# Attention between the products of an MLP: stages emitted job by job, and by pairs of jobs with shared PSUM banks

## The chip, the cores and the metric

The kernel runs on one core of a Trainium2 chip. The metric is the device time of one execution in microseconds, the median of three runs. TensorE (PE) multiplies matrices into PSUM banks, VectorE (DVE) and ScalarE (ACT) read them, GpSimd (POOL) works on SBUF alone, and SyncE (SP) issues most loads and stores.

## The reference

Three parts, one after the other. q, k and v are (4, 8, 576, 64), that is 4 batches of 8 heads; the token matrix has 2304 rows of 512.

```python
# attention: a coarse one on means of 4 positions, plus a local one in a band
out_d = sm_attn(q_d, k_d, v_d)              # q_d, k_d, v_d: mean over 4 positions, 144 of them
out_up = np.repeat(out_d, 4, axis=2)
mask = np.abs(pos[:, None] - pos[None, :]) < 4
scores = np.where(mask, scale * q @ k.T, -1e9)
x = out_up + softmax(scores) @ v
# MLP: 512 -> 2048 -> 512
h = x @ w_in
g = np.maximum(h, 0.0) + np.log1p(np.exp(-np.abs(h)))
x = g @ w_out
# mixture of 8 experts: each token goes to the one with the highest logit
out[mask] = gate_w * (np.maximum(x[mask] @ w1[e], 0.0) @ w2[e])
```

## The kernel before

**Tiling.** The MLP goes over six blocks `n` of 384 tokens, each with 16 chunks `c` of 128 hidden columns. `mlp_H(n, c)` makes the hidden chunk in one PSUM bank `ph` (12 products of 128x128 by 128x384, since both operands are split into a high and a low part; block 0 uses four float32 products). ScalarE takes Abs, Exp and Ln of it, `mlp_g` makes `g` on VectorE and splits it, and `mlp_Y` adds 12 products into the four banks `py`, three iterations later (`step_Y(3)`). `split_wi` and `split_wo` split the weights for the next iteration on ScalarE and GpSimd. Behind block 5 follow the experts, which the change doesn't touch.

**Attention** is cut into 64 jobs, 16 for each batch: four times a `Down` job (the coarse attention of two heads) and a `Local` job (192 positions of the band, two heads), then eight `Local` jobs. Each job has six stages: `st_T` (transposes of q and k, on VectorE from batch 1 on; also issues loads for later jobs), `st_S` (scores into a bank `pS`, L204 to L216 and L303 to L320; VectorE masks and takes the maximum), `st_E` (exponentials on ScalarE), `st_N` (normalising, VectorE and GpSimd), `st_Ta` (transposes into a bank `pA`, VectorE copies it out) and `st_PV` (values into a bank `pO`, L245 to L253 and L341 to L369; the result is copied to `od` by ScalarE for a Down job, and added to `od` by VectorE for a Local job, which writes the MLP's input `xT`).

**Shapes on TensorE.** Local scores are twelve recorded products of 64 rows by 64 columns, Local values twelve of 70 by 64, Down values eight of 72 by 64, Down scores six of 128 by 96. Transposes are of 128 by 70 or 96 by 72. The MLP's are of 128 by 128.

**Order.** A list `pieces` (L393 to L404) holds every stage of every job by steps: at step s the job s starts, job s-2 makes its scores, s-3 its exponentials, s-4 is normalised, s-6 transposed, and s-7 makes its values. Nineteen steps are emitted before the MLP starts. Then `attn_to` emits up to a position in this list twice in each iteration, once behind `mlp_H` and once behind `mlp_Y`; `targets` (L841) says which job's values end in which block. Each block needs the `xT` of its tokens from jobs emitted before.

The order of emission is a priority. A planner with a model of the engines' times sets each engine's instructions in order when the program is built, and may draw one that it thinks ready ahead of one that it thinks not. On the chip every engine keeps that order.

**Banks.** Once the MLP runs, `pa` gives every stage its own bank of the pool `psa` (four banks), which also holds `ph`.

Of the kernel before, what the change touches and what calls it, by code (L numbers as in the profile page):

```python
# [9 lines left out]
F32 = mybir.dt.float32  # L10
# [12 lines left out]
SD = S // FACTOR  # L23
# [9 lines left out]
QD = SD // 3  # L33
# [15 lines left out]
C0 = 3  # L49
CR = 1  # L50
# [5 lines left out]
def band_attention__softplus_mlp__top1_moe(  # L56
# [64 lines left out]
    class Down:  # L121
# [83 lines left out]
        def st_S(self):  # L205
            mx = apool.tile([2 * QD, 3], F32, tag="dmx", name="dmx", bufs=3)
            self.den = apool.tile([2 * QD, 3, 1], F32, tag="dsm", name="dsm", bufs=3)
            ps = pa("pS")
            for i in range(3):
                T.matmul(ps[:2 * QD, i * SD:(i + 1) * SD], self.qbd[:, i, :], self.kT, start=True, stop=True)  # L210
            p3 = ps[:2 * QD, :3 * SD].rearrange("p (i s) -> p i s", i=3)
            V.tensor_reduce(out=mx, in_=p3, axis=AX.X, op=ALU.max, negate=True)
            self.mx, self.p3 = mx, p3
            self.late = not started[0]
            if not self.late:
                self.exps()  # L216
# [28 lines left out]
        def st_PV(self):  # L245
            ps = pa("pO")
            for h, c in pairs(2):
                T.matmul(ps[h * D:(h + 1) * D, :SD], self.vs[:, c, h, :], self.aT[c][:, :, h, :],  # L248
                         start=(c == 0), stop=(c == 1))
            warm(ps)  # L250
            if self.b not in od:
                od[self.b] = apool.tile([128, NPAIR, SD], F32, tag="od", name="od", bufs=1)
            (A.copy if nloc[0] < 99 else V.tensor_copy)(od[self.b][:, self.hp, :], ps[:, :SD])  # L253
# [12 lines left out]
    def pa(name):  # L266

        if not started[0]:
            nps[0] += 1
            if nps[0] % 2:  # L270
                return psy.tile([128, 512], F32, tag="py", name=name)
        return psa.tile([128, 512], F32, tag="pa", name=name)
# [9 lines left out]
    class Local:  # L282
# [20 lines left out]
        def st_S(self):  # L303
            ps = pa("pS")
# [9 lines left out]
            p3 = ps[:, :3 * KW].rearrange("p (i s) -> p i s", i=3)  # L314
# [26 lines left out]
        def st_PV(self):  # L341
            ps = pa("pO")
# [3 lines left out]
            warm(ps)  # L346
            t0 = self.b * S + self.j * TH
# [52 lines left out]
    step_end = {}  # L400
    for s in range(NJ + LAG):
        step_end[s] = sum(1 for x in pieces if x[0] <= s or x[1] < 0)
    pieces.sort(key=lambda x: x[1] >= 0)
    pre_end = [sum(1 for x in pieces if x[0] <= s and (x[1] < 0 or not 0)) for s in range(NJ + LAG)]  # L404
    pos = [0]

    def attn_to(p):
        while pos[0] < min(p, len(pieces)):
            s, n, st = pieces[pos[0]]
            pos[0] += 1  # L410
            with ahead([0, 0, 0, 0, 0, 0][st]):
                (jobs[n].st_T, jobs[n].st_S, jobs[n].st_E, jobs[n].st_N, jobs[n].st_Ta, jobs[n].st_PV)[st]()
            if st == 0:
                if n + 2 < NJ:
                    with ahead(-50):
                        jobs[n + 2].pre()
                with ahead(0):
                    load_after(n)
# [414 lines left out]
    for st in range(12 + LAG):  # L833
        attn_to(pre_end[st])
        if st >= C0 - 5 + LAG:
            conv_to((st - C0 + 5 - LAG) * CR // 4 + 1)
        if st == 9 + LAG:
            split_wi(0, 0)
    started[0] = True
    CB = cpos[0]  # L840
    targets = [23, 32, 44, 56, 63, 63]  # L841
# [13 lines left out]
    for i, (n, c) in enumerate(seq[:NMLP]):  # L855
        if c == 0:
            p0, p1 = pos[0], step_end[targets[n] + LAG]
# [19 lines left out]
        attn_to(p0 + (p1 - p0) * (2 * c + 1) // (28 if n == 0 else 32))  # L877
# [24 lines left out]
        attn_to(p0 + (p1 - p0) * (2 * c + 2) // (28 if n == 0 else 32))  # L902
# [152 lines left out]
```

## Time and profile before

| | |
|---|---|
| median of 3 runs | 796.02 us (795.82 to 797.77) |
| profiled execution | 799.56 us, of it span 797.8 us |
| TensorE busy | 762.2 us (96%), 4917 products |
| VectorE, ScalarE, GpSimd busy | 553.5, 450.8, 469.3 us |
| mean granted clock of TensorE | 0.962 |

The stages can be read from the starts of the products' lines: attention alone to 74.5 us, block 0 of the MLP to 183.6, then blocks 1 to 5 to 262.9, 355.1, 446.1, 520.3 and 586.6, and the experts to the end. Times in a trace count from the start of the span. A group in the view in order of time is a run of instructions of one line; its duration goes to the end of its last instruction, and the next group starts earlier, as products are pipelined. So a group's cost is read from its start to the next group's start.

### The profile page before, as it was taken

Reading aid. Unit: us, or ns where it says so; the run is one execution under the profiler, and the core shown is the slowest. Engines: PE = TensorE matmul, PEld = TensorE weight load, DVE = VectorE, ACT = ScalarE, POOL = GpSimd, SP = SyncE. Lnnn points to the kernel's source line nnn. Section 1 sums busy time; section 2 is a strip of 40 time slices with the busy share of each in tenths; the row PEclk is TensorE's granted clock in tenths of the full one; section 3 lists DMA queues with packets and bytes.
Section 4 is the critical chain, followed back from the end, with each engine's and each line's share of the span. In section 5 each row is a group of like instructions: output and inputs, shape, how many; then the busy total and the mean of one; then the engine's idle time right before and its main releaser. Section 6 shows DMA issues by size and latency. Waiting matters only on the chain.

```text
span 797.8 us, 13867 instructions
## 1 busy us (share of the span) xinstructions
PE 762.2 (96%) x4917; PEld 666.7 (84%) x4918; DVE 553.5 (69%) x1107; ACT 450.8 (57%) x1164; POOL 469.3 (59%) x447
## 2 busy tenths in 40 slices
PE   5997999899999999999999999999999999999995
PEld 5864655578899989899899999999988889889884
DVE  6778999967987587998665665656998285264322
ACT  5734665666476565657565666555665365355332
POOL 3254713656866566876576657666669555555632
PEclk9665999999999999999999999999999999999998
DMA  8757766503300061301000100071012022001002
GB/s 188 153 112 215 231 196 189 119 13 91 62 12 16 24 124 31 72 12 62 2 12 12 52 2 1 1 288 43 1 39 80 21 60 80 0 1 67 14 0 83
DMA packets 111447, 55.46 MB, mean 70 GB/s; under 512 B 89593, under 2 KB 102411, under 8 KB 111371
## 3 DMA queue, kind: packets, MB, share of 16 engines
q1 hardware_dynamic: 111083, 53.98, 25.4%
q8 instruction: 41, 0.67, 0.4%
q10 hardware_dynamic: 288, 0.52, 0.2%
q14 instruction: 35, 0.29, 0.1%
HBM read 45.05 MB, written 9.44 MB: 68 GB/s over the span
## 4 chain that ended last, share of the span: by engine, by line
PE 70%; DVE 16%; issue 4%; DMA 3%; POOL 3%; ACT 2%; SPq 1%; DVEq 0%; ACTq 0%
PE py L622 18%; PE ph L582 17%; PE py L939 11%; PE ph L783 9%; PE pO L344 3%; PE ph L579 3%; PE pS L311 2%; PE pA L336 2%; DVE cva L442 2%; PE pS L210 1%; DVE g L604 1%; DVE xs L764 1%; PE pO L248 1%; DMA vr<-in_v_dram 1%; DVE cva L440 1%
## 5 line engine op out<-in xcount | busy, mean ns | idle before, releaser
L622 PE MATMUL py<-g,wos 128*128 128x384 f32 x1056 | 211.7, 343 | 5.9 <-POOL g L605 2.4
L622 PEld LDWEIGHTS py<-g,wos 128*128 128x128 f32 x1056 | 183.0, 189 | 13.2 <-issue 4.0
L582 PE MATMUL ph<-xT,wis 128*128 128x384 f32 x960 | 183.9, 338 | 0.0
L582 PEld LDWEIGHTS ph<-xT,wis 128*128 128x128 f32 x960 | 166.3, 188 | 2.0 <-issue 0.4
L479 POOL TENSOR_TENSOR wos<-wo,wos 128x512 fp32r<-128x512 f32 x88 | 124.4, 1413 | 42.6 <-ACT wos L478 42.4
L479 POOL TENSOR_TENSOR wis<-wi,wis 128x512 fp32r<-128x512 f32 x80 | 107.3, 1341 | 51.8 <-ACT wis L478 47.5
L588 ACT ACTIVATE ga<-ph 128x384 f32<-128x384 f32 x96 | 46.7, 487 | 77.2 <-PE ph L582 65.2
L603 DVE SCALAR_TENSOR_TENSOR ga<-ph,ga 128x384 f32<-128x384 f32 x88 | 48.3, 549 | 44.8 <-ACT ga L590 44.5
L783 PE MATMUL ph<-xs,ws 128*128 128x384 f32 x378 | 74.3, 337 | 0.9 <-DVE u L788 0.9
L325 ACT ACTIVATE ls<-ls,lst 128x70 f32<-128x70 f32 x144 | 49.3, 344 | 45.4 <-DVE lst L319 33.4
L788 DVE TENSOR_TENSOR u<-ph,u 128x384 f32<-128x384 f32 x60 | 33.2, 555 | 59.1 <-PE ph L783 58.6
L478 ACT CAST wos<-wo 128x512 fp32r<-128x512 f32 x88 | 54.1, 616 | 33.6 <-PE py L622 32.0
L783 PEld LDWEIGHTS ph<-xs,ws 128*128 128x128 f32 x378 | 67.4, 188 | 4.7 <-DVE u L788 1.6
L939 PE MATMUL py<-wos,gs 128*128 128x512 f32 x270 | 68.9, 393 | 0.4 <-POOL gs L794 0.4
L605 DVE TENSOR_TENSOR g<-ga,g 128x384 fp32r<-128x384 f32 x80 | 65.7, 821 | 1.5
L331 POOL TENSOR_TENSOR ls<-ls,lst 128x210 f32<-128x210 f32 x48 | 31.5, 657 | 56.3 <-DVE lst L330 31.2
L604 DVE CAST g<-ga 128x384 fp32r<-128x384 f32 x80 | 57.8, 722 | 4.3 <-PE py L622 0.9
L939 PEld LDWEIGHTS py<-wos,gs 128*128 128x128 f32 x270 | 50.1, 188 | 9.2 <-POOL gs L794 0.8
L479 POOL TENSOR_TENSOR wos<-w2s,wos 128x512 fp32r<-128x512 f32 x24 | 32.7, 1364 | 35.4 <-ACT wos L478 35.4
L590 ACT ACTIVATE ga<-ga 128x384 f32<-128x384 f32 x96 | 50.3, 524 | 2.1
L589 ACT ACTIVATE ga<-ga 128x384 f32<-128x384 f32 x96 | 50.4, 525 | 0.4
L478 ACT CAST wis<-wi 128x512 fp32r<-128x512 f32 x80 | 48.9, 611 | 0.4 <-PE ph L582 0.4
(165 smaller groups left out, 1311.7 us busy)
## 6 DMA issues: line engine op xcount, KB each, us to landing
raw<-in_moe_w_in_dram SPq DMA_DIRECT2D x16, 512.0 KB
raw<-in_moe_w_out_dram SPq DMA_DIRECT2D x16, 512.0 KB
lv<-in_v_dram SPq DMA_DIRECT2D x72, 70.0 KB
vr<-in_v_dram SPq DMA_DIRECT2D x16, 288.0 KB
ydram<-y SPq DMA_DIRECT2D x12, 384.0 KB
yb<-ydram SPq DMA_DIRECT2D x12, 384.0 KB
out_dram<-ob SPq DMA_DIRECT2D x16, 256.0 KB
qr<-in_q_dram SPq DMA_DIRECT2D x48, 72.0 KB
```

The costliest lines, as they stand in the source:

```text
L325: A.activation(s[:, i, :], s[:, i, :], AF.Exp, bias=st[:, 0, i], accum_out=st[:, 1, i])
L478: A.copy(w[:, 0], src)
L479: G.tensor_tensor(out=w[:, 1], in0=src, in1=w[:, 0].bitcast(F32), op=ALU.subtract)
L582: T.matmul(ps[:, :TB], wt[:, w, cc, :], xT[n][:, x, cc, :], start=(i == 0), stop=(i == 3 * CC - 1))
L589: A.activation(a, a, AF.Exp, scale=-1.0)
L590: A.activation(a, a, AF.Ln, bias=1.0)
L603: V.scalar_tensor_tensor(a, ps[:, :TB], 0.0, a, ALU.max, ALU.add)
L604: (A.copy if n < 1 else V.tensor_copy)(g[:, 0, :], a)
L605: (G if n < 1 else V).tensor_tensor(out=g[:, 1, :], in0=a, in1=g[:, 0, :].bitcast(F32), op=ALU.subtract)
L622: T.matmul(yps[n][dc][:, :TB], w[:, a, dsl], g[:, b, :], start=(c == 0 and i == 0), stop=(c == NC1 - 1 and i == 2))
L783: T.matmul(ps[:, :TB], ops[:, w, a, cc, :], xop[p, x][:, l, cc, :], start=i == 0, stop=i == 5)
L939: T.matmul(yps[n][t], g[:, a, t * 128:(t + 1) * 128], w[:, b, :], start=first and c == q and i == 0, stop=last and c == q + NQ and i == 2)
```

## The change

`st_S` and `st_PV` are cut in two: the products stay, and what reads them goes into `st_S2` and `st_PV2`. Up to step 19 the order is the same, with the second halves directly behind the first. From there on a stage's place is given by its pair of jobs (`n // 2`) and a slot: start 0.4, scores 1.0, normalising 1.4, transposing 1.7, values 2.0. At a whole number t come the values of both jobs of pair t-2, the scores of both jobs of pair t-1, then the readers of the values, the readers of the scores and the exponentials. `pa2` gives both jobs of a pair one bank, columns from 0 and from 256: for values always, for scores where both jobs are Local. `ends` replaces `targets`, as slot times at which the blocks begin and end.

```diff
         def st_S(self):                      # Down
-            mx = apool.tile([2 * QD, 3], F32, tag="dmx", name="dmx", bufs=3)
-            self.den = apool.tile([2 * QD, 3, 1], F32, tag="dsm", name="dsm", bufs=3)
             ps = pa("pS")
             for i in range(3):
                 T.matmul(ps[:2 * QD, i * SD:(i + 1) * SD], self.qbd[:, i, :], self.kT, start=True, stop=True)
-            p3 = ps[:2 * QD, :3 * SD].rearrange("p (i s) -> p i s", i=3)
+            self.p3 = ps[:2 * QD, :3 * SD].rearrange("p (i s) -> p i s", i=3)
+
+        def st_S2(self):
+            mx = apool.tile([2 * QD, 3], F32, tag="dmx", name="dmx", bufs=3)
+            self.den = apool.tile([2 * QD, 3, 1], F32, tag="dsm", name="dsm", bufs=3)
+            p3 = self.p3
             V.tensor_reduce(out=mx, in_=p3, axis=AX.X, op=ALU.max, negate=True)
...
         def st_PV(self):                     # Down and Local alike
-            ps = pa("pO")
+            ps = pa2("pO", jobs.index(self), CS)
...
             warm(ps)
+            self.po = ps
+
+        def st_PV2(self):
+            ps = self.po
...
         def st_S(self):                      # Local
-            ps = pa("pS")
+            n = jobs.index(self)
+            ps = pa2("pS", n, CS + LAG if isinstance(jobs[n - n % 2], Local) else NJ)
...
             warm(ps)
-            p3 = ps[:, :3 * KW].rearrange("p (i s) -> p i s", i=3)
+            self.ps = ps
+
+        def st_S2(self):
+            p3 = self.ps[:, :3 * KW].rearrange("p (i s) -> p i s", i=3)
...
-    step_end = {}
-    for s in range(NJ + LAG):
-        step_end[s] = sum(1 for x in pieces if x[0] <= s or x[1] < 0)
-    pieces.sort(key=lambda x: x[1] >= 0)
-    pre_end = [sum(1 for x in pieces if x[0] <= s and (x[1] < 0 or not 0)) for s in range(NJ + LAG)]
+    head = CS + LAG
+    slot = {0: (0.4, 4), 1: (1.0, 1), 2: (1.0, 3), 3: (1.4, 0), 4: (1.7, 0), 5: (2.0, 0)}
+    tail = []
+    for s, n, st in pieces:
+        if s >= head:
+            at, order = slot[st]
+            tail.append((n // 2 + at, order, n, st))
+            if st in (1, 5):
+                tail.append((n // 2 + at, 2, -st, n, st + 5))
+    tail.sort()
...
+    def pa2(name, n, since):
+
+        if n < since:
+            return pa(name)
+        if n % 2:
+            return shared.pop((name, n // 2))[:, 256:]
+        shared[name, n // 2] = pa(name)
+        return shared[name, n // 2]
...
-    targets = [23, 32, 44, 56, 63, 63]
+    ends = [CS / 2 + 2, (16 + 8) / 2 + 1, 17.9, 23.9, 29.9, 33.4, 34.0]
...
-            p0, p1 = pos[0], step_end[targets[n] + LAG]
+            p0, p1 = ends[n], ends[n + 1]
...
-        attn_to(p0 + (p1 - p0) * (2 * c + 1) // (28 if n == 0 else 32))
+        attn_time(p0 + (p1 - p0) * (2 * c + 1) / (28 if n == 0 else 32))
...
-        attn_to(p0 + (p1 - p0) * (2 * c + 2) // (28 if n == 0 else 32))
+        attn_time(p0 + (p1 - p0) * (2 * c + 2) / (28 if n == 0 else 32))
```

Here `CS` is 12 and `LAG` is 7. `attn_time(t)` emits everything whose slot time is not above t.

## Rows read from the trace of the kernel before

**Rows 1.** The page's first part: each engine's busy time, share, instructions.

```profile
PE 762.2 (96%) x4917; PEld 666.7 (84%) x4918; DVE 553.5 (69%) x1107; ACT 450.8 (57%) x1164; POOL 469.3 (59%) x447
```

**Rows 2.** Busy time by stage: stretch, its length, PE, PEld, DVE, ACT, POOL, clock, DMA.

```profile
74.50:183.60 109.10, 103.94 (x622) 67.21 (x621) 100.56 (x217) 66.37 (x191) 56.73 (x53) 0.98 0.54 151
183.60:262.90 79.30, 77.80 (x557) 72.16 (x555) 61.90 (x127) 50.70 (x138) 57.68 (x55) 1.00 0.21 43
262.90:355.10 92.20, 90.81 (x719) 83.50 (x716) 77.70 (x158) 57.26 (x166) 64.32 (x66) 1.00 0.28 57
...
520.30:586.60 66.30, 66.30 (x386) 65.13 (x385) 50.11 (x74) 43.87 (x89) 42.18 (x31) 1.00 0.28 100
```

**Rows 3.** TensorE's waits: line, waited for, us in total, times, longest.

```profile
PE ph L579 <- DVE ls L317: 1.2, 1, 1.2
```

**Rows 4.** TensorE in order of time: start, us, engine, line, tiles, count.

```profile
331.70 0.58 PE L311 MATMUL pS<-qkT 64*64 64x70 f32 x12 [0.34 <-DVE ga L603]
332.21 2.36 PE L622 MATMUL py<-g,wos 128*128 128x384 f32 x12
334.41 2.25 PE L582 MATMUL ph<-xT,wis 128*128 128x384 f32 x12
336.59 0.57 PE L344 MATMUL pO<-laT,lv 70*64 70x64 f32 x12
337.09 0.52 PE L336 MATMUL pA<-ident,ls 128*70 128x128 f32 x3
337.36 0.94 PE L622 MATMUL py<-g,wos 128*128 128x384 f32 x4
...
349.91 2.37 PE L582 MATMUL ph<-xT,wis 128*128 128x384 f32 x12
352.12 2.24 PE L622 MATMUL py<-g,wos 128*128 128x384 f32 x12
354.20 0.49 PE L336 MATMUL pA<-ident,ls 128*70 128x128 f32 x3
```

**Rows 5.** The same view in windows so short that a group's last pairs show.

```profile
343.32 0.29 PE L311 MATMUL pS<-qkT 64*64 64x70 f32 x4
...
343.38 0.23 PE L311 MATMUL pS<-qkT 64*64 64x70 f32 x2
...
343.54 0.57 PE L344 MATMUL pO<-laT,lv 70*64 70x64 f32 x12
```

**Rows 6.** The same view: first and last narrow group, lone transposes.

```profile
78.53 0.57 PE L344 MATMUL pO<-laT,lv 70*64 70x64 f32 x12
...
515.32 0.49 PE L336 MATMUL pA<-ident,ls 128*70 128x128 f32 x3
515.56 4.27 PE L622 MATMUL py<-g,wos 128*128 128x384 f32 x23
519.77 0.57 PE L344 MATMUL pO<-laT,lv 70*64 70x64 f32 x12
```

**Rows 7.** Groups by line, 183.6 to 446 us: busy, mean ns | idle before.

```profile
L605 DVE TENSOR_TENSOR g<-ga,g 128x384 fp32r<-128x384 f32 x48 | 38.3, 798 | 0.8
L604 DVE CAST g<-ga 128x384 fp32r<-128x384 f32 x48 | 37.7, 784 | 1.8 <-PE py L622 0.2
L603 DVE SCALAR_TENSOR_TENSOR ga<-ph,ga 128x384 f32<-128x384 f32 x49 | 26.8, 547 | 17.1 <-ACT ga L590 16.9
...
L329 DVE TENSOR_SCALAR lst<-lst 128x3 f32<-128x3 f32 x23 | 9.1, 396 | 6.5 <-ACT ls L325 6.3
L319 DVE TENSOR_REDUCE lst<-ls 128x3 f32<-128x210 f32 x24 | 8.7, 361 | 0.2
L317 DVE SCALAR_TENSOR_TENSOR ls<-pS,mask 128x210 f32<-128x210 f32 x23 | 8.5, 371 | 15.6 <-PE pS L311 8.2 <-PE pA L336 7.1
...
L330 DVE RECIPROCAL lst<-lst 128x3 f32<-128x3 f32 x23 | 4.0, 172 | 0.5
...
L479 POOL TENSOR_TENSOR wos<-wo,wos 128x512 fp32r<-128x512 f32 x48 | 66.2, 1380 | 23.5 <-ACT wos L478 23.4
...
L331 POOL TENSOR_TENSOR ls<-ls,lst 128x210 f32<-128x210 f32 x23 | 13.4, 584 | 18.8 <-DVE lst L330 13.9 <-ACT wis L478 3.7 <-PE pA L239 0.4
```

More of the change, by code (lines that the diff above doesn't have):

```diff
@@ L49 @@
 C0 = 3
+CS = 12
 CR = 1
@@ L210, in st_S @@
                 T.matmul(ps[:2 * QD, i * SD:(i + 1) * SD], self.qbd[:, i, :], self.kT, start=True, stop=True)
[L211 removed]
+            self.p3 = ps[:2 * QD, :3 * SD].rearrange("p (i s) -> p i s", i=3)
[3 more added lines that the diff above has]
+            p3 = self.p3
             V.tensor_reduce(out=mx, in_=p3, axis=AX.X, op=ALU.max, negate=True)
[L213 removed]
+            self.mx = mx
             self.late = not started[0]
@@ L341, in st_PV @@
         def st_PV(self):
-            ps = pa("pO")
+            ps = pa2("pO", jobs.index(self), CS)
             for h, i in pairs(3):
@@ L346, in st_PV, with st_PV2 @@
             warm(ps)
+            self.po = ps
+        def st_PV2(self):
+            ps = self.po
             t0 = self.b * S + self.j * TH
@@ L399, in band_attention__softplus_mlp__top1_moe, with attn_time @@
         pieces += [(s, n, st) for _, st, n in sorted(at)]
-    step_end = {}
-    for s in range(NJ + LAG):
-        step_end[s] = sum(1 for x in pieces if x[0] <= s or x[1] < 0)
-    pieces.sort(key=lambda x: x[1] >= 0)
-    pre_end = [sum(1 for x in pieces if x[0] <= s and (x[1] < 0 or not 0)) for s in range(NJ + LAG)]
+    head = CS + LAG
[8 more added lines that the diff above has]
+    tail.sort()
+    tail = [(x[0], x[-2], x[-1]) for x in tail]
+    pieces = [x for x in pieces if x[0] < head]
+    pieces = [y for s, n, st in pieces for y in ([(s, n, st), (s, n, st + 5)] if st in (1, 5) else [(s, n, st)])]
+    pre_end = [sum(1 for x in pieces if x[0] <= s) for s in range(head)]
+    pieces += tail
+    times = [x[0] for x in tail]
+    def attn_time(t):
+        attn_to(pre_end[-1] + sum(1 for x in times if x <= t + 1e-6))
+    shared = {}
+    def pa2(name, n, since):
[5 more added lines that the diff above has]
+        return shared[name, n // 2]
     pos = [0]
@@ L410, in attn_to @@
             pos[0] += 1
-            with ahead([0, 0, 0, 0, 0, 0][st]):
-                (jobs[n].st_T, jobs[n].st_S, jobs[n].st_E, jobs[n].st_N, jobs[n].st_Ta, jobs[n].st_PV)[st]()
+            with ahead(0):
+                j = jobs[n]
+                (j.st_T, j.st_S, j.st_E, j.st_N, j.st_Ta, j.st_PV, j.st_S2, None, None, None, j.st_PV2)[st]()
             if st == 0:
@@ L832, in band_attention__softplus_mlp__top1_moe @@
     load_after(-1)
-    for st in range(12 + LAG):
+    for st in range(CS + LAG):
         attn_to(pre_end[st])
```

## The prediction

> **What bounds the kernel now.** I read the page's first part, then the busy time by stage, then TensorE's instructions in order of time, and last the waits and the costs of one instruction on the other engines. TensorE is busy 762.2 of 797.8 us, more than 200 us ahead of any other engine [rows 1]. [...] Block 0 is different: VectorE is busy 100.6 of 109.1 us (it converts weights there) and TensorE 103.9, so it has 5.2 us of idle. The sum is therefore made on TensorE's order of work; the other engines count where they delay it.
>
> The busy time hides what the change is about: a product that only starts later than it could still reads as busy. The start times show it [rows 4]. Twelve full products (128 rows and columns) that neither follow nor precede narrow ones take 2.08 us from their start to the next start (352.12 to 354.20). The twelve at 334.41 have full products before and a narrow group (70 rows by 64 columns) behind, and take 2.18: entering a narrow group costs 0.10. Those at 332.21 and 349.91 follow a narrow group and take 2.20 and 2.21: leaving costs 0.12 there. Leaving costs inside the narrow group too [rows 5]: pairs of score products start 0.06 apart (343.32, 343.38), but the next group starts 0.16 after the last pair, though it is a value group, as narrow as scores but of other rows; so 0.10 for a change between two kinds of narrow group. An exit to full products costs both, 0.22 us. Behind value products, the transposes take 0.27 (337.09 to 337.36) instead of 0.24 (515.32 to 515.56) [rows 4, 6], so that step costs 0.10 and 0.03.
>
> [...]
>
> **The changes of array mode, before and after.** From 74.5 to 586.6 us I count on TensorE 73 entries into narrow groups (the first at 78.53, the last at 519.77), 46 exits to full products, 18 steps from scores to values and 27 from values to transposes (the entries' first and last rows are in [rows 6]). Their price is 73 x 0.10 + 46 x 0.22 + 18 x 0.10 + 27 x 0.13 = 7.3 + 10.1 + 1.8 + 3.5 = 22.7 us.
>
> After the change the emitted order makes one burst of a pair: both jobs' values, then both jobs' scores of the pair behind. A burst of two Local pairs has one entry, one step and one exit: 0.42 us. Where the scores are those of a Down and a Local job, the Down scores (128 rows by 96 columns) stand between, one more change: 0.10 + 0.13 + 0.10 + 0.22 = 0.55. From the slots, pair 6's values to pair 31's, there are 11 bursts of that kind, 13 of the first, and two with values alone (0.32): 6.1 + 5.5 + 0.6 = 12.2 us. Nothing else of the products changes: the same products of the same shapes. The transposes of a pair stand alone, which costs nothing (0.24 for the three). If the order on the chip is the emitted one the saving is 22.7 - 12.2 = 10.5 us. It is not quite, because the program's planner already moves products that it thinks not ready behind others (the trace has such places: twelve products of one half cut in two). Bounds: 10.5 when no burst is torn, 0 when the planner tears them into as many groups as now, and -6 when nothing adjoins any more (91 groups of scores and values at 0.32 are 29). I take 8, near the upper end, because today's emission already keeps single groups whole.
>
> **Block 0.** The attention emitted there goes back: before, scores run up to job 29 and values to job 25, after, to 25 and 23. On VectorE that takes at least four score reads (0.371 + 0.361 us each [rows 7]), 2.9 us, out of the one block where it is full. TensorE's idle there, 109.10 - 103.94 = 5.2 us, is the most that can come back; 0 the least, if the idle comes from the weights' loads; a loss is excluded, as nothing is added to this block. I take 2, nearer to the 2.9 that VectorE is freed of. The moved products reappear in block 1, where VectorE is busy 61.9 of 79.3 us: on TensorE this nets to nothing, and on VectorE it is covered by that slack; without it 2.9 us would be paid there.
>
> **Edits at nothing.** Reading a bank behind both jobs' products delays the first job's read by one group, some 0.5 us [rows 4], hidden by the 4.2 us (twice 2.08) of full products of an iteration, which need none of it. Without that cover it is 0.5 x 26 = 13 us. PSUM: a pair of Local jobs now takes four banks in turn from the pool of four where it took six, so the products wait no more for a bank than now; a bank is held longer, but until two reads instead of one. Loads: those of a Down job are still issued with the start of a job some three places ahead, on SyncE's queue, now about two pairs before use instead of one and a half; the value windows' loads keep three buffers and now live 1.6 pairs instead of 7 jobs. Neither is on the path, as TensorE waits for no load from block 0 on; if a load came late, a pair's values would wait for it.
>
> **The added waits.** From start to values a job now takes 1.6 pairs, where it took 7 jobs, 3.5 pairs. A pair lasts about 92.2 / 6 = 15.4 us in block 2 [rows 2], so the 0.3 of a pair from normalising to transposing, and again from transposing to values, is 4.6 us each. Normalising has to do, for both jobs: VectorE 2 x (0.396 + 0.172), 1.1 us, behind one iteration's 0.547 + 0.784 + 0.798 = 2.1; then GpSimd 2 x 0.584 behind one weight subtract of 1.38: 2.5 us [rows 7]. That is 5.7 us against 4.6. What waits: the transposes on TensorE and, queued behind them, the MLP's products; SyncE has nothing behind. The planner sees this and sets full products ahead of them; what remains are its errors. Bounds: 1.1 us in each of 26 bursts, 29 us, and below nothing, a gain of 3: today VectorE waits 7.1 us for transposes to free a buffer of masked scores [rows 7], which their shorter life ends, and TensorE can get back from it no more than its idle of blocks 1 and 2, 1.5 and 1.4 us [rows 2]. The nearest row is today's waiting for attention's readers, for example 1.2 us once for the mask step [rows 3], so waits are rare; I take 0.1 us a burst, 2 us.
>
> **Sum.** 8 + 2 - 2 = 8 us less than the profiled execution's own time of 799.56 (span 797.8 and 1.8 around it): 791.6. The median shown, 796.02, is 0.9956 of that execution, so 788 us.
>
> **Rivals.**
> 1. *The short chain is felt (slower).* Place: the transposes, 0.3 of a pair behind the normalising. If every second burst waits the full 1.1 us that the sum above is late, 13 x 1.1 = 14 us are added to -10: 799.56 + 4 = 803.6, by the same ratio 800. It decides from 10 / 26 = 0.4 us a burst. For it: VectorE is busy 77.7 of 92.2 us in block 2, and two reads, two reduces, copies and casts now come in one heap before the MLP's own. Against it: the MLP's second half is held three iterations back, so there are full products to put in. [...]
> 2. *The change doesn't do what it says.* The planner tears the bursts, because a pair's second job is often late, and the count of mode changes stays near 160. Then only block 0 gains, less the waits: about 796, the same.
> 3. *More.* The whole 10.5, all of block 0's 5.2 and the idle of blocks 1 and 2 vanish, since buffers come free earlier: 10.5 + 5.2 + 2.9 = 18.6 less, 781, so 777.5 by the ratio. Against: idle of block 0 that comes with the weights' loads stays.
>
> **How the numbers follow.** The forecast has 0.58 (785 to 793), rival 1 0.16, rival 2 0.16, rival 3 0.10. A measurement here tells 0.3%, 2.4 us, from no change. Faster: 0.58 and 0.10, and a quarter of rival 2: 0.72. Same: most of rival 2 and the tail of rival 1: 0.13. Slower: 0.15. The range 780 to 800 leaves out the extreme of rival 3 and the upper half of rival 1, together under 0.2.
>
> **What would show it.** Right: on TensorE, groups of 24 value products with 24 score products directly behind; the count of entries near 37 (15 bursts with one, 11 with two) instead of 73, and hardly a step from values to transposes instead of 27; blocks 2 and 3 some 2 us shorter each, at the same granted clock; block 0 shorter by more than its moved work. Wrong: TensorE's waits name the normalising (GpSimd, ls or de) or the copies of transposes; groups of 12 as before; block 0's VectorE no less full.

## The result, and the profile after

The changed kernel takes 798.55 us (median of 22 runs, 793.39 to 807.42) and the kernel before, on the same chip, 793.22 us (22 runs, 789.49 to 797.77). The ratio is 1.0066, 95% interval 1.0041 to 1.0092: slower, where I had forecast 788 us and faster. (The forecast started from 796.02 us, the median of the three runs that I had; over 22 runs the kernel before takes 793.22. The ratios here and below are taken over the runs and need not be the quotient of the two medians.)

The one profiled execution of each tells the opposite: 794.17 us after (span 792.3), 799.56 before. So the first thing to read in this pair is where the two spans differ. Busy time by stage, the kernel after (stretch, its length, then PE, PEld, DVE, ACT and POOL busy, granted clock, DMA); the rows are the stretch ahead of block 0, the blocks 0 to 3, block 5 and the experts:

```profile
0.00:63.40 63.40, 45.17 (x441) 36.96 (x443) 52.84 (x119) 37.74 (x141) 28.35 (x56) 0.92 0.85 203
63.40:166.60 103.20, 97.94 (x535) 64.26 (x534) 89.90 (x192) 63.10 (x171) 45.10 (x42) 0.96 0.46 132
166.60:254.40 87.80, 84.33 (x619) 78.99 (x618) 65.17 (x141) 51.30 (x139) 63.57 (x65) 0.98 0.31 61
254.40:346.40 92.00, 88.48 (x696) 81.78 (x695) 62.88 (x146) 55.72 (x165) 61.56 (x62) 1.00 0.23 47
346.40:436.80 90.40, 88.05 (x686) 81.69 (x684) 63.46 (x149) 54.27 (x162) 57.97 (x55) 1.00 0.12 29
...
511.80:579.90 68.10, 68.10 (x397) 66.93 (x396) 52.95 (x75) 45.20 (x91) 43.02 (x32) 1.00 0.24 88
579.90:792.30 212.40, 199.43 (x987) 177.15 (x985) 105.45 (x178) 95.31 (x181) 113.93 (x94) 0.98 0.12 42
```

The same view of the kernel before, its stretch ahead of block 0, block 3 and the experts (blocks 0, 1, 2 and 5 are in [rows 2]):

```profile
0.00:74.50 74.50, 58.56 (x441) 47.35 (x443) 52.63 (x119) 38.47 (x141) 28.11 (x56) 0.68 0.71 160
355.10:446.10 91.00, 91.00 (x713) 84.24 (x710) 60.16 (x144) 54.96 (x161) 57.56 (x53) 1.00 0.07 19
586.60:797.80 211.20, 199.57 (x987) 177.03 (x985) 105.58 (x178) 95.18 (x181) 114.28 (x94) 0.98 0.12 42
```

And the stretch ahead of block 0 in a second profiled execution of the kernel before:

```profile
0.00:66.60 66.60, 49.52 (x441) 39.81 (x443) 52.99 (x119) 37.91 (x141) 28.34 (x56) 0.85 0.78 178
```

Ahead of block 0 nothing was changed, and yet it takes 74.5, 66.6 and 63.4 us, in the order of the mean granted clock, 0.68, 0.85 and 0.92. That scatter is larger than everything that the change did, so spans of single executions say nothing here. From the first product of block 0 to the first of the experts it is another matter: 512.1 and 512.3 us in the two executions before, 516.5 after. With the experts (211.2 and 211.4 before, 212.4 after) that is 5.2 to 5.6 us more; the medians differ by 5.3. This stretch of 512 us is used below and called the middle.

TensorE's idle is the length less the PE column. Before it was 5.2 us in block 0, 1.5 and 1.4 in blocks 1 and 2 [rows 2] and none in block 3. After it is 5.3 in block 0, 3.5, 3.5 and 2.4.

TensorE's waits ahead of the local transposes and of `py` products, after (line, waited for, us in total, times, longest):

```profile
PE pA L348 <- POOL ls L343: 7.2, 2, 6.7
...
PE py L665 <- DVE g L647: 6.0, 5, 1.7
PE py L665 <- POOL wos L522: 3.0, 2, 2.8
PE py L665 <- DVE g L648: 2.9, 3, 1.1
```

The same lines before:

```profile
PE pA L336 <- POOL ls L331: 5.2, 1, 5.2
PE py L622 <- POOL g L605: 2.4, 2, 1.7
...
PE py L622 <- DVE g L604: 1.6, 1, 1.6
...
PE py L622 <- DVE g L605: 1.1, 1, 1.1
...
PE py L622 <- ACT wos L478: 0.6, 1, 0.6
...
PE py L622 <- POOL wos L479: 0.2, 1, 0.2
```

`py` products waited 5.9 us for the MLP's own operands before, 11.9 after. The one long wait for attention's normalising (`ls`), 5.2 us before and 6.7 after, stands just ahead of block 0 in both kernels; in blocks 1 to 3 the transposes wait 0.9 us in all. What is late there is not attention's normalising but `g` and the weights' split, the MLP's side.

TensorE in order of time, after (start, us, line, tiles, count): a burst as it was meant, and one pair later torn in two.

```profile
329.63 0.92 PE L356 MATMUL pO<-laT,lv 70*64 70x64 f32 x24
330.48 0.95 PE L320 MATMUL pS<-qkT 64*64 64x70 f32 x24
331.36 2.38 PE L625 MATMUL ph<-xT,wis 128*128 128x384 f32 x12
...
360.42 0.57 PE L356 MATMUL pO<-laT,lv 70*64 70x64 f32 x12
360.92 0.98 PE L209 MATMUL pS<-dkT,dbd 128*96 128x144 f32 x6
361.63 2.17 PE L665 MATMUL py<-g,wos 128*128 128x384 f32 x11
363.74 0.57 PE L356 MATMUL pO<-laT,lv 70*64 70x64 f32 x12
364.24 0.58 PE L320 MATMUL pS<-qkT 64*64 64x70 f32 x12
```

At 329.63 both jobs' values and both jobs' scores stand together, 24 and 24, with one entry, one step and one exit. At 360.42 one job's values come with a Down job's scores; eleven full products follow, and then the other job's values and scores. Entries into narrow groups fell from 73 to 45, where I had expected 37. Steps from values to transposes fell from 27 to 1.

For the totals I took each product's start to the next start, set aside what an undisturbed product of its shape takes (2.08 us / 12 for a full one, [rows 4]), put what is over it at a change of shape to mode changes, at most the prices of the prediction, and the rest to waiting. In the middle:

| | mode changes | waiting | of it block 0, blocks 1 to 3 | middle |
|---|---|---|---|---|
| before | 20.4 | 15.7 | 8.7, 5.8 | 512.3 |
| after | 14.4 | 26.6 | 10.7, 14.8 | 516.5 |

So 6.0 us of mode changes are gone, and 10.9 us of waiting have come.

Not all of this waiting is idle time. The longest wait of the middle, after, with what follows it (TensorE in order of time, then busy time, where the first figure behind the engines is the granted clock):

```profile
213.64 3.68 PE L665 MATMUL py<-g,wos 128*128 128x384 f32 x12 [2.75 <-POOL wos L522]
```

```profile
214.30:217.70 3.40, 3.02 (x10) 2.51 (x8) 0.84 (x3) 1.04 (x2) 3.40 (x5) 0.50 0.00 0
```

TensorE was idle for 2.75 us, then the granted clock was 0.50 for 3.4 us, and twelve full products took 3.68 us, where [rows 4] has 2.24 to 2.37. The same stands in block 0, from 115.3 to 118.7 us, behind an idle of 2.19 us. In the kernel before, neither trace has such a stretch in blocks 1 to 3, and one of the two has one in block 0, behind an idle of 1.67 us. Each of the three traces also has a stretch at 0.50 that reaches into the start of block 0 (to 78.5 us in the first trace before, to 67.5 after). Worked out from the starts of the products in these stretches, the half clock takes 5.0 us of the middle after and 2.0 and 2.2 in the two traces before. So some 3 of the 10.9 us are products at the half clock, and TensorE's idle grew by 6.6 us (8.1 to 14.7).

### The profile page after: what moved, and what is told of

The parts are those of the page before. It is cut to its first block, busy times and chain, and to the rows that moved or that the text cites. A ratio compares the mean times of both kernels' runs of the same rounds, so it can differ in the third digit from the quotient of the medians.

```text
span 792.3 us, 13885 instructions
## 1 busy us (share of the span) xinstructions
PE 746.5 (94%) x4917; PEld 660.1 (83%) x4918; DVE 544.5 (69%) x1107; ACT 448.8 (57%) x1164; POOL 462.2 (58%) x447
## 4 chain that ended last, share of the span: by engine, by line
PE 69%; DVE 18%; ACT 4%; issue 3%; DMA 3%; SPq 1%; POOL 1%; DVEq 0%; ACTq 0%; POOLq 0%
PE py L665 17%; PE ph L625 17%; PE py L982 12%; PE ph L826 10%; PE ph L622 3%; DVE g L647 2%; PE pS L320 2%; PE pO L356 2%; DVE cva L485 2%; PE pA L348 1%; DVE g L648 1%; PE py L662 1%; DVE xs L807 1%; DVE ga L646 1%; PE pS L209 1%
## 5 line engine op out<-in xcount | busy, mean ns | idle before, releaser
L665 PEld LDWEIGHTS py<-g,wos 128*128 128x128 f32 x1056 | 184.2, 190 | 20.6 <-issue 4.5
L826 PE MATMUL ph<-xs,ws 128*128 128x384 f32 x378 | 74.5, 338 | 0.0
L521 ACT CAST wos<-wo 128x512 fp32r<-128x512 f32 x88 | 54.4, 618 | 27.3 <-PE py L665 23.0
L648 DVE TENSOR_TENSOR g<-ga,g 128x384 fp32r<-128x384 f32 x80 | 68.2, 853 | 1.7
L647 DVE CAST g<-ga 128x384 fp32r<-128x384 f32 x80 | 54.8, 685 | 4.5 <-PE py L665 1.1
L343 POOL TENSOR_TENSOR ls<-ls,lst 128x210 f32<-128x210 f32 x48 | 28.2, 592 | 36.3 <-DVE lst L342 21.7
```

Source lines behind the costliest of these rows:

```text
L521: A.copy(w[:, 0], src)
L647: (A.copy if n < 1 else V.tensor_copy)(g[:, 0, :], a)
L648: (G if n < 1 else V).tensor_tensor(out=g[:, 1, :], in0=a, in1=g[:, 0, :].bitcast(F32), op=ALU.subtract)
L665: T.matmul(yps[n][dc][:, :TB], w[:, a, dsl], g[:, b, :], start=(c == 0 and i == 0), stop=(c == NC1 - 1 and i == 2))
L826: T.matmul(ps[:, :TB], ops[:, w, a, cc, :], xop[p, x][:, l, cc, :], start=i == 0, stop=i == 5)
```

## The experiments

Fourteen kernels ran, each timed against the kernel before on the same chip, but for the kernel before itself, once more, which gave its second trace. Four questions came one after the other: is it the shared bank, is it heaps of work, is it the short chain, and if so at which of its steps. Then a table of pairing by chain length, and one copy that runs on ScalarE.

**The kernel before, unchanged.**

> The kernel before, unchanged, for a second trace. In the first pair of traces, from block 0's first product to the experts' first, the kernel before took 512.1 us and the changed one 516.6, while the stretch ahead of block 0 differed by 11 us with the granted clock (74.5 us at 0.5 to 1.0 before, 63.4 at 0.6 to 1.0 after). Theory W (waits): the order of the changed kernel costs TensorE some 11 us of new waits in blocks 1 to 3 and gives back 6 us of array-mode changes; then this trace shows the body again at 511 to 514 us with about 16 us of waits, whatever the clock ahead of it. Rival N (noise): the body of the kernel before scatters by 4 us or more between executions; then it lands near 516.

Measured: 792.12 us in one execution; its middle is within 0.2 us of the other trace's.

**Own banks for every stage.**

```diff
-        if n < since:
+        if n >= 0:
             return pa(name)
```

> The changed kernel with a bank of its own for each job's scores and values; the order of emission is the same. Theory S (shared banks): the readers of the first job wait for the second job's products and ScalarE's and VectorE's reads of one bank go one after the other, which makes VectorE's heap late; then this is 3 to 8 us faster than the changed kernel, 791 to 795 where the kernel before takes 793. Theory W (short chain and heaps): sharing is harmless, so 797 to 801, or slower still if four banks run short.

Measured: 800.72 us, ratio 1.0099 (1.0067 to 1.0130); waiting 34.7, mode changes 17.1. Without sharing it is not faster, so nothing here says that the shared bank and its readers' turns are the cost. Own banks can bring a cost of their own, a shortage of the four, so a small price of sharing is not excluded by this run alone; the short chain without pairs, below, has the loss with no bank shared.

**The pair's starts, exponentials and score readers spread over the slots.**

```diff
-    slot = {0: (0.4, 4), 1: (1.0, 1), 2: (1.0, 3), 3: (1.4, 0), 4: (1.7, 0), 5: (2.0, 0)}
+    slot = {0: (0.2, 4), 1: (1.0, 1), 2: (1.2, 3), 3: (1.4, 0), 4: (1.7, 0), 5: (2.0, 0)}
...
+            at += 0.4 * (st == 0 and n % 2)
...
-                tail.append((n // 2 + at, 2, -st, n, st + 5))
+                tail.append((n // 2 + at + 0.2 * (st == 1), 2, -st, n, st + 5))
```

> The changed kernel with VectorE's heaps spread: the start of the even job at 0.2 and of the odd job at 0.6 pairs (both 0.4 before), the readers of scores and the exponentials at 1.2 instead of 1.0; products and banks as in the changed kernel. Theory H (heaps): waits of TensorE for the second half of the MLP's activation (g) and for split weights fall back, 4 to 8 us, so 791 to 795. Theory C (short chain): exponentials now have 0.2 pair less ahead of normalising, so it is the same or slower, 798 to 804.

Measured: 798.73 us, ratio 1.0107 (1.0069 to 1.0146); waiting 28.8. Spreading the heaps in this way wins nothing.

**The chain lengthened, still by pairs** (values at 3.0 instead of 2.0, one more buffer of masked scores, blocks' ends one pair later).

```diff
-            s = apool.tile([128, 3, KW], F32, tag="ls", name="ls", bufs=3)
+            s = apool.tile([128, 3, KW], F32, tag="ls", name="ls", bufs=4)
...
-    slot = {0: (0.4, 4), 1: (1.0, 1), 2: (1.0, 3), 3: (1.4, 0), 4: (1.7, 0), 5: (2.0, 0)}
+    slot = {0: (0.4, 4), 1: (1.0, 1), 2: (1.0, 3), 3: (1.6, 0), 4: (2.2, 0), 5: (3.0, 0)}
...
-    ends = [CS / 2 + 2, (16 + 8) / 2 + 1, 17.9, 23.9, 29.9, 33.4, 34.0]
+    ends = [CS / 2 + 3, (16 + 8) / 2 + 2, 18.9, 24.9, 30.9, 34.4, 35.0]
```

> The changed kernel with the chain stretched: normalising at 1.6 instead of 1.4 pairs, transposing at 2.2 instead of 1.7, values at 3.0 instead of 2.0, the blocks' limits moved by one pair so that values end where they ended, and one more buffer of masked scores. The bursts (values of a pair, then scores of a later pair) stay. Theory C (short chain): the new waits come from 0.3 pair between steps; with 0.6 and 0.8 they go, some 6 to 9 us, so 790 to 793, faster than before. Theory H (heaps: both jobs' readers and q and k transposes on VectorE at one place): the heaps are as they were, so 796 to 800.

Measured: 792.14 us, ratio 0.9992 (0.9965 to 1.0018). The loss is gone. Waiting in blocks 1 to 3 is 7.7 us, mode changes 12.3. Only block 0 had become longer, 114.3 us, and 5.6 us of that stood at its start, where TensorE waited for a copy of transposes. That is not an added cost: the wait for normalising just ahead of block 0, 5.2 us before and 6.7 in the changed kernel, is gone here, and TensorE's idle ahead of block 0 is 11.6 us, against 18.2 in the changed kernel. So the two kernels differ in the chain, with about the same wait at the start, and their intervals lie apart.

**The same with block 0's attention begun 0.9 of a pair earlier in the slots' count.**

```diff
-    ends = [CS / 2 + 3, (16 + 8) / 2 + 2, 18.9, 24.9, 30.9, 34.4, 35.0]
+    ends = [CS / 2 + 2.1, (16 + 8) / 2 + 2, 18.9, 24.9, 30.9, 34.4, 35.0]
```

> The long chain run with the first limit at 8.1 pairs instead of 9. In the long chain run block 0 took 114 us against 109 before, with 5.6 us of wait at its start for the values of jobs 12 and 13, whose transposes are emitted in the same call; here these have 0.8 pair between them. Theory: the wait at the start goes and block 0 loses 4 to 8 us, so 785 to 789, under both kernels. Rival: block 0 is bound by VectorE's conversion of the weights, the wait only moves, 791 to 793.

Measured: 788.67 us, ratio 0.9963 (0.9936 to 0.9990): faster than both kernels. In this trace neither wait at the start is left; the longest there is 2.1 us. So the gain over the run above (0.3%, with intervals that overlap) goes with the start of block 0, not with the chain. Busy time by stage of this kernel, blocks 1 to 3:

```profile
169.90:253.80 83.90, 81.38 (x599) 77.15 (x598) 64.93 (x137) 51.72 (x141) 61.16 (x61) 0.98 0.25 53
253.80:345.30 91.50, 89.46 (x704) 83.54 (x704) 74.03 (x154) 54.44 (x163) 61.22 (x63) 0.98 0.28 56
345.30:432.10 86.80, 86.80 (x689) 82.04 (x688) 63.28 (x145) 55.13 (x164) 55.94 (x55) 1.00 0.07 20
```

TensorE is idle 2.5, 2.0 and 0 us in blocks 1 to 3, against 3.5, 3.5 and 2.4 in the changed kernel. And in order of time the pair that was torn there at 360.42 is whole, all its values ahead of its scores:

```profile
360.22 0.92 PE L356 MATMUL pO<-laT,lv 70*64 70x64 f32 x24
361.07 0.98 PE L209 MATMUL pS<-dkT,dbd 128*96 128x144 f32 x6
361.98 0.58 PE L320 MATMUL pS<-qkT 64*64 64x70 f32 x12
362.49 1.16 PE L665 MATMUL py<-g,wos 128*128 128x384 f32 x5
```

**The short chain without pairs** (job by job, every stage in its own bank).

```diff
-            tail.append((n // 2 + at, order, n, st))
+            tail.append((n / 2 + at, order, n, st))
...
-        if n < since:
+        if n >= 0:
```

The readers' line has `n / 2` as well, and the ends follow the odd jobs' half pair: 8, 13.5, 18.4, 24.4, 30.4, 33.9, 34.0.

> The changed kernel with the pairing undone and the short chain kept: each job has its own place (half its number plus the slot, so an odd job comes half a pair later) and its own bank; the blocks' limits are half a pair later so that values end in the same half iteration. With the kernel before (single jobs, long chain), the changed one (pairs, short chain) and the long chain run (pairs, long chain: 792.1 against 792.6 for the kernel before) this fills the square. Theory C (the short chain costs, the pairing gains): the waits of blocks 1 to 3 stay near 15 us as in the changed kernel, where the kernel before has 6, and the array-mode changes come back towards 20 us from 14; 798 to 805. Rival P (pairs cost, whatever the chain): waits fall to the 6 us of before, 790 to 794.

Measured: 797.66 us, ratio 1.0073 (1.0046 to 1.0101). Mode changes are back at 20.6, as before the change, and waiting is 21.7. By stage, blocks 1 to 3:

```profile
176.10:258.10 82.00, 79.23 (x580) 73.04 (x578) 65.05 (x135) 50.73 (x145) 59.74 (x62) 1.00 0.34 66
258.10:352.60 94.50, 92.18 (x715) 84.71 (x714) 70.70 (x152) 54.07 (x156) 59.64 (x62) 0.98 0.22 45
352.60:443.70 91.10, 91.10 (x698) 82.92 (x697) 61.03 (x149) 57.16 (x170) 58.51 (x57) 1.00 0.13 29
```

2.8, 2.3 and 0 us of idle against 1.5, 1.4 and 0 before. So the new emission with the short chain, without any pair, costs about what the whole change costs. Pairing on top of it saves 6.2 us of mode changes and adds 4.9 of waiting.

**Only one of the two steps lengthened.** First up to the transposes (with four buffers of masked scores, ends as in the long chain), then from the transposes to the values (with four buffers of transposes):

```diff
-    slot = {0: (0.4, 4), 1: (1.0, 1), 2: (1.0, 3), 3: (1.4, 0), 4: (1.7, 0), 5: (2.0, 0)}
+    slot = {0: (0.4, 4), 1: (1.0, 1), 2: (1.0, 3), 3: (1.4, 0), 4: (2.7, 0), 5: (3.0, 0)}
```

> Pairs, with all the stretch between normalising and transposing: normalising 1.4, transposing 2.7, values 3.0 (one more buffer of masked scores). Theory C1 (the transposes, behind VectorE and GpSimd, are what comes late, as the prediction's rival had it): as good as the long chain run, 790 to 794, waits of blocks 1 to 3 at 6 to 9 us. Theory C2 (the values, behind the copies of the transposes, come late): as the changed kernel, 796 to 800, waits near 15.

```diff
-    slot = {0: (0.4, 4), 1: (1.0, 1), 2: (1.0, 3), 3: (1.4, 0), 4: (1.7, 0), 5: (2.0, 0)}
+    slot = {0: (0.4, 4), 1: (1.0, 1), 2: (1.0, 3), 3: (1.4, 0), 4: (1.7, 0), 5: (3.0, 0)}
```

> Pairs, with all the stretch between transposing and values: normalising 1.4, transposing 1.7, values 3.0 (one more buffer of transposed weights). Theory C1 (the transposes come late): as the changed kernel, 796 to 800, waits of blocks 1 to 3 near 15 us. Theory C2 (the values come late): 790 to 794, waits at 6 to 9.

Measured: 798.36 us, ratio 1.0086 (1.0049 to 1.0122), and 795.06 us, ratio 1.0040 (1.0014 to 1.0067). Waiting in blocks 1 to 3 is 16.3 and 12.1 us. Neither step alone gives the whole loss back. The second comparison is not clean, though: in that trace 4.4 us of wait stand at the start of block 0 on top of 6.2 just ahead of it, and the changed kernel has only the latter (6.7 us).

**A fourth buffer of `g`** (and three instead of four buffers of a Down job's transposes, for the room), in the changed kernel and, as a control, in the one before.

```diff
-        g = mlp.tile([128, 2, TB], F32R, tag="g", name="g", bufs=3)
+        if 0 < n < NB - 1 and c % 4 == 3 and c < 12:
+            g = apool.tile([128, 2, TB], F32R, tag="gx", name="g", bufs=1)
+        else:
+            g = mlp.tile([128, 2, TB], F32R, tag="g", name="g", bufs=3)
```

> The changed kernel with a fourth buffer for the MLP's activation g in blocks 1 to 4 (every fourth chunk up to the twelfth uses one of the attention's pool; the room comes from one buffer less of the Down jobs' transposes). In the traces a product of the MLP's second half starts a median 3.1 to 3.4 us behind the end of its g in blocks 2 and 3 of the changed kernel, against 6.5 to 8.0 with the long chain. Theory G (the planner fills the places where attention isn't ready with the MLP's second half, and so uses up its lead over g): with one more g in flight the lead grows and the waits on g go, of the 14.8 us of waits in blocks 1 to 3 some 5; 792 to 795. Rival Q (what is late is late on VectorE and GpSimd whatever the lead): same as the changed kernel, 796 to 800.

> The kernel before with the same fourth buffer, as the control: it has 5.8 us of waits in blocks 1 to 3, of which about 2 us name g. Theory G: 0 to 2 us faster, 790 to 792. Rival Q: the same as the kernel before, 791 to 793.

Measured: 796.68 us, ratio 1.0064 (1.0032 to 1.0095), and 791.95 us, ratio 1.0006 (0.9974 to 1.0038). No difference from either kernel: `g` is not late for want of a buffer. That VectorE comes to it late is what rival Q says; this run does not show it.

**A Down job's values copied by VectorE** instead of ScalarE, in the changed kernel.

```diff
-            (A.copy if nloc[0] < 99 else V.tensor_copy)(od[self.b][:, self.hp, :], ps[:, :SD])
+            (A.copy if nloc[0] < 4 else V.tensor_copy)(od[self.b][:, self.hp, :], ps[:, :SD])
```

> The changed kernel with the copy of a Down job's values to od on VectorE instead of ScalarE from the second batch on; VectorE then adds od into the MLP's input on its own queue, with no handoff. In the changed kernel VectorE is idle 10.5 us (4 times) in blocks 1 to 3 for that handoff, in the kernel before never. Theory F (this handoff, made late by the short chain and the shared bank, is what the short chain costs): the 10.5 us of VectorE's idle go, TensorE's waits in the body fall from 26.6 to about 20, and the time falls by 4 to 6 us, ratio to before 0.999 to 1.002. Theory C (the short chain leaves no slack on all of its steps, the handoff is one symptom): the idle goes, VectorE takes over 12 copies, TensorE's waits stay within 4 us of 26.6, ratio 1.004 to 1.009.

Measured: 794.65 us, ratio 1.0016 (0.9994 to 1.0038). Most of the loss is gone by this one line, though not by the mechanism that I had named. VectorE's idle ahead of the copy or the add, blocks 1 to 3, in the changed kernel and then in this one:

```profile
DVE xf L376 <- ACT od L261: 10.5, 4, 4.3
```

```profile
DVE od L261 <- PE pO L356: 10.2, 5, 3.6
```

The idle stays; it only has the values themselves as its end now. VectorE had come to that place before the products had, and the copy takes 0.31 us on VectorE here (median of 15), where ScalarE's took 0.28 in the changed kernel (median of 16). What is smaller is TensorE's waiting for `g`:

```profile
PE py L665 <- POOL wos L522: 3.0, 2, 2.7
PE py L665 <- DVE g L647: 2.3, 2, 1.6
...
PE py L665 <- DVE g L648: 2.0, 3, 1.0
```

TensorE is idle 3.2, 2.3 and 0.6 us in blocks 1 to 3, against 3.5, 3.5 and 2.4. Whether that follows from the copy's place or from the order that the planner gave all the other instructions around it, the two traces don't tell.

**The long chain without pairs**: the edit of the short chain without pairs, with the long slots and four buffers of masked scores, ends 8.1, 14.5, 19.4, 25.4, 31.4, 34.9, 35.0.

> The same emission by slot times and split stages as the changed kernel, but job by job (n / 2), every stage in a bank of its own, and with the long slots (normalising 1.6, transposes 2.2, values 3.0, four buffers of masked scores, the late start of e7). With e4 (job by job, short) it is the other half of a table of pairing by chain length. Theory C (the chain's length is what costs): like the kernel before, ratio 0.998 to 1.002, array-mode changes about 20 us, TensorE's waits in the body about 15. Theory M (the new emission itself, split stages and slot times, costs about 5 us, and the long chain only happens to be placed well with pairs): ratio 1.005 to 1.010, waits over 20.

Measured: 795.31 us, ratio 1.0028 (1.0001 to 1.0055), between the two expectations. Mode changes are 20.7. Waiting is 27.3, but 7.4 of it is one wait at the start of block 0, in the place of the one ahead of block 0; in blocks 1 to 3 it is 9.0. So some 0.3% may belong to the new emission or to that start; this is not settled.

**The copy on VectorE in two more kernels**, the short chain without pairs and the long chain by pairs.

> e4 (job by job, short chain, own banks) with the copy of a Down job's values to od on VectorE. In e4 VectorE was never idle for the handoff od (ScalarE's copy to VectorE's add), yet it measured 1.0073; in the changed kernel the same edit gave 1.0016. Theory P (the handoff comes from the pairing: values of a Down and a Local job together, in one bank, then read by two engines in turn): nothing to win here, ratio 1.005 to 1.010, TensorE's waits about 21. Theory A (ScalarE is relieved of a copy that stands ahead of exponentials or of the MLP's Abs, wherever it stands): ratio 0.999 to 1.004, waits under 18.

> e7 (pairs, long chain, late start) with the copy to od on VectorE. In e7 VectorE is idle 2.1 us for the handoff in blocks 1 to 3, against 10.5 in the changed kernel. Theory P (the handoff costs where pair and short chain meet; the long chain already hides it): ratio 0.994 to 0.999, as e7. Theory A (ScalarE's copy costs anywhere): 0.990 to 0.993, half a per cent under e7.

Measured: 800.26 us, ratio 1.0108 (1.0074 to 1.0141), and 786.82 us, ratio 0.9910 (0.9883 to 0.9937). Each theory is right in one half, the first with a ratio just above its range. Job by job the copy wins nothing. By pairs it wins half a per cent with the short chain, where the intervals lie apart; with the long one it is 0.5% by the ratios and 0.3% by the medians of all runs (786.82 of 792.35 us, against 788.67 of 791.73), and the intervals touch. The last is the best kernel of this study. Its stages, blocks 1 to 3:

```profile
170.40:252.90 82.50, 80.95 (x607) 76.86 (x606) 70.94 (x137) 52.11 (x142) 61.73 (x61) 1.00 0.26 54
252.90:344.30 91.40, 88.96 (x706) 83.46 (x705) 74.43 (x158) 53.83 (x159) 61.48 (x63) 0.98 0.29 57
344.30:430.70 86.40, 86.40 (x687) 81.79 (x686) 62.60 (x150) 54.32 (x160) 56.34 (x55) 1.00 0.07 20
```

1.6, 2.4 and 0 us of idle in blocks 1 to 3, and blocks 2 and 3 are 91.4 and 86.4 us long, against 92.2 [rows 2] and 91.0 before.

**The table that decides**, ratios to the kernel before, all with the new emission:

| | short chain (values at 2.0) | long chain (values at 3.0) |
|---|---|---|
| job by job | 1.0073 (1.0046 to 1.0101) | 1.0028 (1.0001 to 1.0055), start moved |
| by pairs | 1.0066 (1.0041 to 1.0092) | 0.9992 (0.9965 to 1.0018) |
| by pairs, start of block 0 moved | not run | 0.9963 (0.9936 to 0.9990) |
| by pairs, copy on VectorE | 1.0016 (0.9994 to 1.0038) | 0.9910 (0.9883 to 0.9937), start moved |

The waits at the start have to be kept apart. Just ahead of block 0 or at its start the traces have one wait of 5.2 us (short, job by job), 6.7 (short, by pairs), 7.4 (long, job by job) and 5.6 (long, by pairs), but none above 2.1 by pairs where the start was moved. With about the same wait there, the long chain wins 0.74% by pairs, and these intervals lie apart; job by job it wins 0.45%, with 2.2 us more of that wait, and those overlap a little. With the copy on VectorE it wins 1.1%, of which the shorter wait at the start (4.1 us against 1.1) is about 0.4%. Pairing wins nothing at the short chain. At the long one it wins 0.36% where both have such a wait, and the intervals overlap; of the 0.65% that the row with the moved start has over job by job, 5.3 us of that wait are about all. That pairing saves mode changes is shown by the traces (20.7 us against 12.3 at the long chain), and what it is worth in time is not settled. For the chain's length there is more than the one pair of kernels: with ScalarE's copy left in place, the seven kernels with the short chain or one short step, paired or not, lie at 1.0040 to 1.0107, and the three with the long chain at 0.9963 to 1.0028.

## Why the prediction was wrong, point by point

The path was right. TensorE's order of work bounds the kernel, and all that was won or lost stands in its pitch in the middle: -6.0 for mode changes, +10.9 for waiting, -0.7 for the products' own time, +1.0 in the experts, together +5.2; the medians give +5.3.

*Mode changes: right in kind, too large by a quarter.* I took 8 us of a possible 10.5; 6.0 went. Bursts were formed and transposes stand apart (1 step from values instead of 27), but 45 entries remain instead of 37, since pairs are torn. I had laid tearing to the planner's errors as such. The runs show that the chain's length is part of it: with the long chain by pairs 42 entries remain and mode changes come to 12.7 us, close to the 12.2 that the emitted order gave.

*The added waits: the step that failed.* I took 2 us in 26 bursts, 0.1 a burst, from one row of 1.2 us [rows 3], and allowed for up to 29. The waiting grew by 9.0 us in blocks 1 to 3 and 2.0 in block 0. About 3 us of this is the half clock behind the waits, for which the sum had no term: blocks 1 and 2 stood at 1.00 in [rows 2]. The prediction had the shortage itself: 5.7 us of work against 4.6 of room between normalising and transposing. It then let the planner cover it with full products, and that cover is not free. The median time from the end of a Local job's normalising to its transposes, worked out from the starts of all of them in blocks 1 to 3, fell from 22.0 us to about 3 (9 and 11 in the two kernels with the long chain by pairs), and yet TensorE hardly waits at the transposes there, where I would have looked for it: it waits for `g`. As I read it, attention's reads, which used to be done whenever VectorE had room, are now due at once and stand ahead of the MLP's casts in VectorE's order, so the full products that should be the cover are themselves late. The traces bear this out in part. From the end of a chunk's `ph` products to the end of its `g`, in blocks 1 to 3, the median is 5.3 us before and 6.5 after, and every tenth `g` takes over 7.6 and over 10.1: `g` is later. But it is as late with the long chain by pairs and the moved start (5.9, and over 11.4). What differs there is the room behind it: the median time from the end of a `g` to its products, in blocks 2 and 3, is 3.1 and 3.4 us after and 3.4 and 4.2 before, but 6.5 and 8.0 in the first kernel with the long chain by pairs. And the order is not the only thing that makes `g` late: of the 5.4 us that TensorE waits for `g` in blocks 1 to 3, 3.1 stand behind two casts that themselves took 3.84 us (shown in the last section) and 1.45. So the chain's length as the cause is shown, and how it makes the products wait is argued. The row on which I based the 0.1 measured how often attention's readers were late with 22 us of room, which says nothing of how often they are with 3.

*Block 0: none of the 2 us.* TensorE's idle there was 5.2 us and is 5.3. Block 0 is shorter by about 6 us: 5.9 of products that moved to the later blocks and 2.1 of mode changes, less 2.0 of more waiting, about 1.5 of it products at the half clock. VectorE's busy time in it fell from 100.6 to 89.9 us, and no idle of TensorE went with that; less work on VectorE alone does not bring it back.

*Edits at nothing.* Reading behind both jobs' products and the shared banks cost nothing that shows: own banks were not faster, though that run does not exclude a small price. The idle of VectorE for a buffer of masked scores, 7.1 us [rows 7], did go entirely, and TensorE got nothing for it.

*Rival 1* had the direction and the cause, the short chain, and 800 us against 798.55 measured. It was wrong on the place: the wait is not at the transposes. Nor is it at the handoff of a shared bank from ScalarE to VectorE, since banks of their own don't help (1.0099 against 1.0066) and the idle of that handoff (10.5 us) is mostly the wait for the values, which is 10.2 us with the copy on VectorE. That its figure came so near is partly luck: its 14 us of waits and its 10 us of savings were both too large, against 10.9 and 6.0. Its point of decision, 0.4 us a burst, was met: 10.9 / 26 = 0.42. I had given it 0.16. *Rival 2* (torn bursts) holds for a part of the bursts: 45 entries stand nearer to 37 than to 73. *Rival 3* had idle of TensorE vanish as buffers come free; it grew.

What stays open: why moving one copy to VectorE wins 0.3 to 0.5% by pairs and nothing job by job. Kernels with the same short chain by pairs differ by up to 0.4% after edits that won nothing (own banks, spread starts), and the planner sets all engines' orders anew each time; an effect of that size in one pair of kernels is not proof of a mechanism. Here it came twice with pairs, with the same sign. And 0.3% between the kernel before and the long chain without pairs was not traced.

## What to carry to other kernels

When stages are regrouped, count separately what the grouping saves and what the new distance between stages takes: here grouping saved 6 to 8 us of mode changes by the traces, the distance, halved along with it, cost 0.7%, and only kernels with one of the two changed told them apart. Look also at what else such a kernel changes: moving the slots moved a wait of 5 us at the start of block 0, which is as much as pairing was seen to win. A dependent chain that runs beside a bound engine should keep its old length when it is regrouped, and a wait that is rare at a large slack gives no rate for a small one. Look for the price not only at the chain's own waits: on an engine that keeps its order, as VectorE kept the program's for all 1106 of its instructions in the trace after, work that has become urgent can delay the bound engine's other operands; so I read the waits for `g` here, 5.4 us in blocks 1 to 3.

## What the runs showed of the hardware

Beside GpSimd a cast on VectorE took up to 4.53 us here, over ten times the median of 0.41. The casts of `g` (128 partitions by 384, from SBUF to SBUF), after; count: least, median and longest in ns, first and last start:

```profile
L647 DVE CAST g<-ga x80: 320/410/4528, 171.7 to 589.4; 128x384 fp32r<-128x384 f32 x80
```

One of the long ones stands at a wait of TensorE. VectorE, GpSimd and TensorE in order of time, after:

```profile
336.75 3.84 DVE L647 CAST g<-ga 128x384 fp32r<-128x384 f32 x1
340.51 0.64 DVE L331 TENSOR_REDUCE lst<-ls 128x3 f32<-128x210 f32 x2
```

```profile
335.77 1.28 POOL L156 TENSOR_TENSOR vr<-vr 72x512 f32<-72x512 f32 x1 [1.47 <-DMA vr<-in_v_dram]
337.02 1.29 POOL L522 TENSOR_TENSOR wis<-wi,wis 128x512 fp32r<-128x512 f32 x1
338.27 0.87 POOL L159 TENSOR_TENSOR vs<-vr 72x128 f32<-72x128 f32 x2
339.11 1.26 POOL L522 TENSOR_TENSOR wos<-wo,wos 128x512 fp32r<-128x512 f32 x1
340.33 1.40 POOL L522 TENSOR_TENSOR wis<-wi,wis 128x512 fp32r<-128x512 f32 x1
```

```profile
340.73 0.94 PE L665 MATMUL py<-g,wos 128*128 128x384 f32 x4 [1.27 <-DVE g L647]
342.79 0.45 PE L665 MATMUL py<-g,wos 128*128 128x384 f32 x1 [1.12 <-DVE g L648]
```

The cast starts at 336.75, while GpSimd's subtract of 335.77 runs, and ends at 340.59, through four further GpSimd instructions without a gap between them; TensorE then waits 1.27 us for it and 1.12 us for the subtract that follows it. Of the 80 casts of this trace the 23 that ran beside no GpSimd instruction took 0.36 us each, and the 57 that ran beside one a median of 0.72; the two longest, 4.53 and 3.84 us, had GpSimd busy for nearly all of their length, through several of its instructions in a row. In sum the casts are no longer than before: the 80 of the changed kernel took 54.8 us, those of the kernel before 57.8, and in the best kernel of this study, the long chain by pairs with the copy on VectorE, the longest took 6.15 us. No run kept GpSimd away from these casts, so what they cost in all is not measured.

The other thing is the stretch ahead of block 0: the same instructions took 63.4 to 74.5 us in three executions, at a mean granted clock of 0.92 to 0.68. In [rows 2] and in the rows after, the mean clock of a block is 0.96 or more. But such a mean can hide stretches at 0.50: the changed kernel has two of 3.4 us behind the start of block 0, behind an idle of TensorE of 2.19 and 2.75 us, and its products in them took about 1.5 us longer each time.
